# Attention outputs stored by row, the second block's fetch and spread moved behind the last weights, the second group's norms moved later (one core, four alternating layers)

## The chip, the cores and the metric

The kernel runs on one core of a Trainium2 chip. The metric is the device time of one launch in microseconds: the median of 3 runs. A profiled execution gives a page and a trace; its own time is given beside its span. Engines are called as the profile calls them: PE (matrix multiplies), DVE (vector), ACT (scalar activations), POOL (GpSimd), SP (here only an issuer of transfers). A transfer is issued by an engine's queue (SPq, POOLq, ACTq) and runs on 16 DMA engines.

## The reference, cut to what matters

A sequence of 2048 rows of 640 values goes through four layers, A, B, A, B (layer 0 to 3), each on a layer norm of its input and added to it.

```python
x = x + A(layernorm(x)); x = x + B(layernorm(x)); x = x + A(layernorm(x)); x = x + B(layernorm(x))

def A(x):                                   # 32 heads of 192
    for s in range(64):                     # 32 rows each
        h = concat([mem, x[32*s:32*s+32]])  # 8 + 32 rows
        q, k, v = h @ Wq, h @ Wk, h @ Wv
        o = softmax(mask(q k^T * scale)) v  # per head
        o = o @ Wo                          # summed over the heads
        mem = o[:8]; outs.append(o[8:])

def B(x):                                   # 32 heads of 20, over all 2048 rows
    q, k, v = split(x @ wqkv)
    phi(u) = concat(softmax(u @ w_phi), softmax(-u @ w_phi))
    kv = phi(k)^T v;  z = sum(phi(k))
    return (phi(q) kv / (phi(q) z + 1e-6)) @ wo
```

Layer A is sequential: a segment needs `mem` of the one before it. Of its 40 rows, only the first 32 (8 rows of `mem` and 24 outputs) are multiplied by Wo inside this chain. The last 8 rows of each segment, the "tails", feed nothing in the chain, and their product with Wo is made later, for 16 segments (128 rows) at once.

## The kernel before, in words

**Layer A** is a batch part (`A_pre`, the projections of the tail rows) and then the chain (`A_chain`, L918). A segment is worked off in 4 rounds of 8 heads, in the order 0 to 3 in even segments and 3 to 0 in odd ones, so that the weights of the last round serve the next segment's first. Weights stream from HBM on the SP queue: `load_slot` (L683) for Q, K and V, `load_wo` (L700) for the output weights, six pieces of 320 KB for a round. The chain's order is written out by hand (`manual_schedule`); instructions stand on each engine in program order there.

A round's attention (L1039) leaves its output in PSUM, 80 columns for two heads. Columns 0 to 63 are copied to `OT` (L1044 on ACT, L1045 on DVE) and multiplied by the output weights (`wo_round`, L1065). Columns 64 to 79, the tails, are copied by `keep_tail` (L1051 or L1053, and L1054) to `otb`, a tile with two buffers, and stored by `store_tail` (L1058) on the POOL queue: 128 partitions x 96 bf16 values, 24 KB, into `otb_d`, which is [segment, partition, 384]. That is done 4 x 64 times in a chain. The segment's last copies are `keep_rows` (L953, four on ACT), which wait for the result W of the four rounds and keep the 24 output rows.

**The end of the chain.** In segment 63, behind the first `wo_round`, SP issues `fetch_tails` (L1221) for block 0 and block 1 (a block is 16 segments: 128 partitions x 16 x 384 values, 1536 KB), then the six pieces of Wo for the last round, then six pieces of Wo of round 3 that layer B's beginning needs. Behind the last attention, `spread_tails` of block 0 (four copies of 128 x 1536, helper lines L87 on DVE and L89 on ACT) puts the fetched values into the order that the multiply needs. The spread of block 1 belongs to layer B, whose order a scheduler makes; it may place it among the chain's last steps.

**Layer B** (L247 on) begins with these tails: `multiply(tb)` for tb = 0 to 3, each of 48 chunks with a 512-column (L1251) and a 128-column (L1252) matmul; the sums of one block go to `obB` and from there to `attn`. Two buffers hold two blocks in turn, so fetch and spread of tb + 2 follow multiply of tb. Then come four groups of 512 rows (g = 0 to 3):

- `norm_T(g)`: load rows (L350), add the attention (L356, POOL), layer norm (`ln_moments`, `ln_deviation`, `ln_apply`: DVE L222, L224, L226, L240, L242; ACT L233, L234, and L244 for the rows), and turn them by PE (L166) and ACT (L89).
- `keys_values(g)`: for 4 blocks of 128 rows, keys on PE (L410, ps_pk), exponentials on ACT (L424), sums and reciprocals on DVE (L426, L428), values on PE (L410, ps_v), scaled on DVE (L437), and their products summed on PE (L443).
- `query_norms(g - 1)`: PE L473 and L481, ACT L345, L338, L339, DVE L340, L476, L482. `queries(g)`: PE L462, ACT L465.

Group 0's rows are normed and turned between multiply(2) and multiply(3); group 1's `norm_T` is held back by `issue_after` until group 0's last turn. `issue_after(i)` tells the scheduler not to place what follows before instruction i has been issued; it is about the order, not a wait on the chip. After the groups come the attention (PE L561, L564; ACT L566, DVE L567) and the output rows (PE L410 with ps_wo, DVE L596). Layer 1 also norms its output rows for the next layer A: `measure_rows` (the moments) and `finish_rows` (the rest), hung by `issue_after` behind the attention's steps of the next group. Layer 3 has no such norm.

The lines that the change touches are `otb_d` (L653), `store_tail` (L1058), `fetch_tails` (L1221), its calls at L1169, the spread in L493, `norm_T(1)` at L519, and `attention`, `measure_rows`, `finish_rows` and `output_rows` (L554 to L613).

Of the kernel before, what the change touches and what calls it, by code (L numbers as in the profile page):

```python
# [115 lines left out]
class Kernel:  # L116
# [131 lines left out]
    def layer_B(self, x_dram, at_dram, xout_dram, xnext_dram, li, bp, post):  # L248
# [42 lines left out]
        with tc.tile_pool(name=f"B{li}_kv", bufs=1, space=bass.MemoryType.PSUM, reuse_waits="tile") as kvp, \  # L291
# [121 lines left out]
            def keys_values(g, xnT):  # L413
                VS = DH * (512 // DH)

                def tokens(b):
# [3 lines left out]
                def keys(b):  # L420
                    ek = eks.next().rearrange("p (s d) -> p s d", s=2)
                    for ps, lo, hi in pair("ps_pk", 512, KC, tokens(b), lambda k, lo, hi: wqkv[:, k, D + lo:D + hi]):
                        for sg in range(2):
                            nc.scalar.activation(out=ek[:, sg, lo:hi], in_=ps[:, 0:hi - lo], func=ACT.Exp, scale=1.0 - 2.0 * sg)  # L424
                    sk = bp.tile([P, 2 * H], F32, name="sk", tag="sk")
                    nc.vector.reduce_sum(out=sk[:], in_=ek[:, :, :].rearrange("p s (h f) -> p (s h) f", f=DH), axis=AX.X)  # L426
# [22 lines left out]
                for b in range(4 * g, 4 * g + 4):  # L449
                    now = (b, *keys(b))  # L450
                    if before is not None:
                        values(*before)
                    before = now
                values(*before)

# [35 lines left out]
            with tc.issue_after(last.ins):  # L491
                load_rows(0)
            ow.append(spread(1, ot[1]))  # L493
            ot += [fetch(tb) for tb in range(2, 4)]
# [16 lines left out]
            turned = []  # L511
            multiply(3, ow[3], kv_ps[1], side_bank("ps_post"),
                     {35 + 4 * b: lambda b=b: turned.append(turn_rows(b, rows[b], first_xnT)) for b in range(4)})
            turned = turned[-1]
            waiting = None
            for g in range(NG):
                if g == 0:
                    xnT = first_xnT
                elif g == 1:  # L519
                    with tc.issue_after(turned.ins):  # L520
                        xnT = norm_T(g)
                else:
                    xnT = norm_T(g)
                if g == 1:
                    late_constants()
                keys_values(g, xnT)
# [27 lines left out]
            def attention(g, hl):  # L554
                tk = slice(512 * g, 512 * g + 512)
                oT = oTs.next().rearrange("p (c t) -> p c t", c=NC_)
                for c in range(NC_):
                    mc = sizes[c]
                    pn = bank("ps_num")
                    for sg in range(2):  # L560
                        nc.tensor.matmul(pn[0:mc, :], lhsT=kvm[0:mc, sg, c, 0:mc], rhs=phi[0:mc, sg, c, tk], start=(sg == 0),  # L561
                                         stop=(sg == 1))
                    pe = bank("ps_e")
                    nc.tensor.matmul(pe[0:mc, :], lhsT=expc[0:64, c, 0:mc], rhs=hl, start=True, stop=True)  # L564
                    rx = rxs.next()
                    spread = nc.scalar.activation(out=rx[0:mc, :], in_=pe[0:mc, :], func=ACT.Copy)  # L566
                    scaled = nc.vector.tensor_tensor(out=oT[0:mc, c, :], in0=pn[0:mc, :], in1=rx[0:mc, :], op=ALU.mult)  # L567
                    with tc.issue_after(spread.ins), tc.issue_after(scaled.ins):
                        if c in (0, 2):
                            measure_rows()  # L570
                        if c > 1:
                            finish_rows()
                return oT

            written, measured = [], []

            def measure_rows():
                if written:
                    ob, rows = written.pop(0)
                    measured.append((ob, self.ln_moments(bp, ob, 6), rows))  # L580

            def finish_rows():
                if measured:
                    ob, m, rows = measured.pop(0)
                    xn = xns.next()
                    self.ln_apply(bp, ob, m, self.ln_deviation(bp, m), xn, True)
                    nc.gpsimd.dma_start(out=xnext_dram[rows, :], in_=xn[:])

            def output_rows(g, oT):
                for b in range(4 * g, 4 * g + 4):  # L590
# [7 lines left out]
                    if xnext_dram is not None:  # L598
                        written.append((ob, rows))
                        if b < 4 * g + 2:  # L600
                            measure_rows()

            hl = [denominators(0, side_bank), denominators(1, bank)]
            for g in range(NG):
# [5 lines left out]
                output_rows(g, oT)  # L610
            for _ in range(4):
                measure_rows()
                finish_rows()  # L613
# [31 lines left out]
    def layer_A(self, xn_dram, at_dram, li, x_raw=None):  # L645
# [6 lines left out]
        self.vb_d = dram.tile([NSEG, NR, 2, 8, 896], BF16, name=f"vb{li}")  # L652
        self.otb_d = dram.tile([NSEG, P, 384], BF16, name=f"otb{li}")  # L653
        wview = self.wview
# [263 lines left out]
    def A_chain(self, xn_dram, at_dram, li, load_slot, piece, load_wo, late_wo, wo_mid, wo_end, low):  # L918
# [3 lines left out]
        with tc.tile_pool(name=f"A{li}_ch", reuse_waits="tile", bufs=1) as sp, \  # L922
# [28 lines left out]
            def keep_rows(W):  # L951
                for g in range(4):
                    nc.scalar.activation(out=orow[:, 160 * g:160 * g + 160], in_=W[32 * g:32 * g + 32, 0:160], func=ACT.Copy)  # L953

# [93 lines left out]
            def keep_tail(o, late=False):  # L1048
# [3 lines left out]
                else:  # L1052
                    nc.scalar.activation(out=otb[:, 0:3, :], in_=o[0][:, :, 64:80], func=ACT.Copy)  # L1053
                nc.vector.tensor_copy(out=otb[:, 3:6, :], in_=o[1][:, :, 64:80])  # L1054
                return otb

            def store_tail(otb, s, r):
                nc.gpsimd.dma_start(out=self.otb_d[s, :, 96 * r:96 * r + 96], in_=otb[:, :, :].rearrange("p c t -> p (c t)"))  # L1058

# [59 lines left out]
            for s in range(NSEG):  # L1119
# [30 lines left out]
                for n in range(L):  # L1150
# [63 lines left out]
                store_tail(keep_tail(o), s, order[L])  # L1214
# [81 lines left out]
```

## Time and profile before

| | |
|---|---|
| median of 3 runs | 3639.28 us (3635.94, 3639.28, 3642.32) |
| profiled execution | 3645.08 us, span 3643.3 us, mean granted clock 0.986 |
| PE busy | 3508.5 us (96%) |
| DVE, ACT, POOL busy | 2329.6, 2041.1, 1584.8 us (64%, 56%, 43%) |
| DMA | 933.32 MB, 256 GB/s over the span |
| stores L1058 | 512 of 24.0 KB, 4.8 us from issue to landing |
| fetches L1221 | 8 of 1536.0 KB, 12.1 us from issue to landing |
| first multiply of layers 1 and 3 (L1251) | begins at 1560.10 and 3384.7 us |

Each row of the timeline is the start, the length, the engine, the line, the instruction with its output and input, and in brackets how long the engine had been idle before it and what ended that. In a list of waits the numbers are the microseconds in total, how many times, and the longest. PE may be busy and still slow: the granted clock says at which share of full speed it ran. The layers' borders are seen in the slices of the page: the two stretches with hardly any DMA are the layers B.

### The profile page before, as it was taken

Reading aid. Unit: us, or ns where it says so; the run is one execution under the profiler, and the core shown is the slowest. Engines: PE = TensorE matmul, PEld = TensorE weight load, DVE = VectorE, ACT = ScalarE, POOL = GpSimd, SP = SyncE. Lnnn points to the kernel's source line nnn. Section 1 sums busy time; section 2 is a strip of 40 time slices with the busy share of each in tenths; the row PEclk is TensorE's granted clock in tenths of the full one; section 3 lists DMA queues with packets and bytes.
Section 4 is the critical chain, followed back from the end, with each engine's and each line's share of the span. In section 5 each row is a group of like instructions: output and inputs, shape, how many; then the busy total and the mean of one; then the engine's idle time right before and its main releaser. Section 6 shows DMA issues by size and latency. Waiting matters only on the chain.

```text
span 3643.3 us, 168559 instructions
## 1 busy us (share of the span) xinstructions
PE 3508.5 (96%) x70978; PEld 2274.2 (62%) x71269; DVE 2329.6 (64%) x6368; ACT 2041.1 (56%) x5233; POOL 1584.8 (43%) x4149
## 2 busy tenths in 40 slices
PE   9999999999999999989999899999999999999899
PEld 7766666666666666655377566666666666666553
DVE  5456666666666666646543566666666766666464
ACT  3356666666666666646432566666666666666362
POOL 3445555555555545530123445555555555555300
PEclk9999999999999999999899999999999999999998
DMA  9988888887888888860487888888887888888600
GB/s 306 328 292 292 285 281 277 291 295 270 287 292 281 277 281 289 285 207 1 140 270 211 296 272 292 288 278 290 285 288 270 294 291 276 281 293 281 202 1 29
DMA packets 533265, 933.32 MB, mean 256 GB/s; under 512 B 141066, under 2 KB 300442, under 8 KB 532506
## 3 DMA queue, kind: packets, MB, share of 16 engines
q1 hardware_dynamic: 431098, 821.50, 64.7%
q0 software_dynamic: 67744, 87.80, 8.3%
q10 hardware_dynamic: 33664, 13.24, 1.4%
q8 instruction: 557, 9.13, 1.0%
q14 instruction: 202, 1.65, 0.1%
HBM read 852.43 MB, written 73.73 MB: 254 GB/s over the span
## 4 chain that ended last, share of the span: by engine, by line
PE 67%; DMA 11%; issue 8%; DVE 7%; ACT 4%; POOL 2%; SPq 0%; POOLq 0%; DVEq 0%; ACTq 0%
PE ps_qk L989 19%; PE ps_w L1065 8%; PE ps_v L989 8%; DMA arena<-wo_rows 6%; PE ps_pre L880 6%; PE ps_o L1039 5%; PE ps_s L1031 4%; PE ps_pre L904 3%; PE ps_s L1097 3%; DVE hT L945 2%; PE ps_s L1026 2%; PE ps_idle L1072 2%; PE kv L1251 2%; DMA arena<-in_A_Wv_dram 2%; ACT raw L999 2%
## 5 line engine op out<-in xcount | busy, mean ns | idle before, releaser
L989 PEld LDWEIGHTS <-hT 128*32 128x32 bf16 x30720 | 738.2, 96 | 432.2 <-DVE hT L1213 28.4
L989 PE MATMUL ps_qk<-arena,hT 128*32 128x384 bf16 x20480 | 997.4, 327 | 10.6 <-DMA arena<-in_A_Wk_dram 1.8
L999 ACT ACTIVATE raw<-ps_qk 128x384 bf16<-128x384 f32 x1024 | 503.0, 491 | 380.4 <-PE ps_s L1097 241.0
L1065 PE MATMUL ps_w<-arena,OT 128*32 128x160 bf16 x24576 | 547.8, 235 | 52.2 <-DMA arena<-wo_rows 19.9
L972 POOL DMA_DIRECT2D Vp<-vb x512 | 259.1, 506 | 652.0 <-PE ps_o L1039 450.8
L989 PE MATMUL ps_v<-arena,hT 128*32 128x384 bf16 x10240 | 535.4, 329 | 5.9 <-DMA arena<-in_A_Wv_dram 5.9
L1065 PEld LDWEIGHTS <-OT 128*32 128x32 bf16 x24576 | 436.5, 97 | 149.6 <-issue 58.4
L1004 DVE STREAM_TRANSPOSE KT<-raw 128x384 bf16<-128x384 bf16 x512 | 296.1, 578 | 198.4 <-ACT raw L999 194.4
L1007 DVE STREAM_TRANSPOSE QT<-raw 128x256 bf16<-128x256 bf16 x512 | 227.9, 445 | 238.2 <-ACT raw L999 196.6
L960 POOL DMA_DIRECT2D kqb<-kqb x512 | 291.9, 570 | 174.6 <-POOL KT L968 147.3
L1020 DVE CAST Vp<-ps_v 64x384 bf16<-64x384 f32 x512 | 286.1, 559 | 96.2 <-ACT Vp L1018 81.6
L1058 POOL DMA_DIRECT2D otb<-otb x512 | 284.5, 556 | 131.1 <-DVE otb L1054 101.7
L1018 ACT ACTIVATE Vp<-ps_v 64x384 bf16<-64x384 f32 x512 | 246.3, 481 | 151.8 <-PE ps_v L989 114.1
L1045 DVE CAST OT<-ps_o 128x192 bf16<-128x192 f32 x512 | 183.1, 358 | 211.8 <-PE ps_o L1039 193.9
L1104 DVE TENSOR_TENSOR E<-E,ps_s 80x320 bf16<-80x320 bf16 x512 | 247.5, 483 | 73.2 <-ACT ps_s L1103 69.2
L1083 ACT ACTIVATE E<-ps_s 80x320 bf16<-80x320 f32 x512 | 221.9, 433 | 124.7 <-PE ps_s L1031 96.5
L1039 PEld LDWEIGHTS <-Vp 80*128 80x128 bf16 x4096 | 183.5, 99 | 154.4 <-issue 120.1
L1039 PE MATMUL ps_o<-E,Vp 80*128 80x80 bf16 x4096 | 233.8, 202 | 22.2 <-ACT Vp L1018 3.8
L1044 ACT ACTIVATE OT<-ps_o 128x192 bf16<-128x192 f32 x512 | 167.8, 328 | 146.1 <-PE ps_o L1039 146.1
L1031 PE MATMUL ps_s<-QT,KT 128*80 128x80 bf16 (+1 forms) x3072 | 232.7, 213 | 11.9 <-DVE KT L1004 3.4
L953 ACT ACTIVATE Vp<-ps_w 32x160 bf16<-32x160 f32 x512 | 150.7, 294 | 166.4 <-DVE wt L1212 151.2
L1072 PE MATMUL ps_idle<-arena,ident 128*128 128x230 bf16 (+1 forms) x1792 | 236.3, 260 | 0.0
(151 smaller groups left out, 5182.1 us busy)
## 6 DMA issues: line engine op xcount, KB each, us to landing
arena<-wo_rows SPq DMA_DIRECT2D x792, 320.0 KB, 6.9
arena<-in_A_Wq_dram SPq DMA_DIRECT2D x427, 384.0 KB, 4.6
arena<-in_A_Wv_dram SPq DMA_DIRECT2D x427, 384.0 KB, 6.4
arena<-in_A_Wk_dram SPq DMA_DIRECT2D x768, 192.0 KB, 4.9
kqb<-kqb POOLq DMA_DIRECT2D x512, 48.0 KB, 5.1
arena<-in_A_Wk_dram SPq DMA_DIRECT2D x43, 384.0 KB, 7.4
vb<-arena POOLq DMA_DIRECT2D x128, 112.0 KB, 6.0
Vp<-vb POOLq DMA_DIRECT2D x512, 28.0 KB, 4.8
```

Of the source, the lines that this page charges most:

```text
L960: nc.gpsimd.dma_start(out=kqb[:], in_=self.kqb_d[s, :, r, :])
L972: nc.gpsimd.dma_start(out=Vs[n % 2][64:80, :], in_=self.vb_d[s, r].rearrange("g t f -> (g t) f"))
L989: nc.tensor.matmul(o[32 * g:32 * g + 32, 0:384], lhsT=hT[:, b, :], rhs=rhs, start=(i == 0), stop=(i == KC - 1), tile_position=(0, 32 * g), ...
L999: nc.scalar.activation(out=raw[:], in_=ps[:, 0:384], func=ACT.Copy)
L1004: nc.vector.transpose(out=KT[:, :, 0:64], in_=raw[:, :].rearrange("p (c j) -> p c j", j=64))
L1020: nc.vector.tensor_copy(out=o, in_=i)
L1031: nc.tensor.matmul(S[0:80, c0:c0 + 80 * (q1 - q0)], lhsT=KT[:, 3 * x + i, :], rhs=QT[:, x, q0:q1, :], start=False, stop=(x == 1 and i == 2 ...
L1039: nc.tensor.matmul(O[x][:, 80 * i:80 * i + 80], lhsT=Vs[n % 2][0:80, 448 * x + k:448 * x + k + 128], rhs=E[0:80, 160 * x + 80 * e:160 * x ...
L1058: nc.gpsimd.dma_start(out=self.otb_d[s, :, 96 * r:96 * r + 96], in_=otb[:, :, :].rearrange("p c t -> p (c t)"))
L1065: nc.tensor.matmul(W[32 * g:32 * g + 32, 0:160], lhsT=OT[:, c, q:q + 32], rhs=w[:, 640 * i + 160 * g:640 * i + 160 * g + 160], start=(firs ...
L1072: nc.tensor.matmul(ps[:, 0:w], lhsT=self.ident[:, :], rhs=wo_mid[:, 0:w], start=True, stop=True, skip_group_check=True)
L1104: nc.vector.tensor_tensor(out=E[0:80, 0:320], in0=E[0:80, 0:320], in1=rc, op=ALU.mult)
```

## The change

Four edits.

1. `otb_d` is laid out [partition, segment, 384]. A store's 128 pieces of 192 bytes then stand 49,152 bytes apart, where they stood 768 apart. A fetch reads 128 runs of 12,288 bytes, where it read 2048 of 768.
2. The fetch of block 1 stands on the SP queue behind all twelve pieces of Wo. The spread of block 1 is placed behind the chain's last tail copy on DVE and the last copy of `keep_rows` on ACT.
3. `norm_T(1)` is held until the last exponential and the last sum of group 0's second block, not only until group 0's last turn.
4. The norm of layer 1's output: the moments follow the output rows directly, the rest of the norm follows each attention step from the second on, with no `issue_after`, and what is left is done at the end.

```diff
-            ow.append(spread(1, ot[1]))
+            with tc.issue_after(self.chain_end[0].ins), tc.issue_after(self.chain_end[1].ins):
+                ow.append(spread(1, ot[1]))
...
                 elif g == 1:
-                    with tc.issue_after(turned.ins):
+                    with tc.issue_after(self.second_block[0].ins), tc.issue_after(self.second_block[1].ins):
                         xnT = norm_T(g)
...
-                    with tc.issue_after(spread.ins), tc.issue_after(scaled.ins):
-                        if c in (0, 2):
-                            measure_rows()
-                        if c > 1:
-                            finish_rows()
+                    if c > 0:
+                        finish_rows()
...
-                        written.append((ob, rows))
-                        if b < 4 * g + 2:
-                            measure_rows()
+                        unfinished.append((ob, self.ln_moments(bp, ob, 6), rows))
...
-            for _ in range(4):
-                measure_rows()
+            while unfinished:
                 finish_rows()
...
-        self.otb_d = dram.tile([NSEG, P, 384], BF16, name=f"otb{li}")
+        self.otb_d = dram.tile([P, NSEG, 384], BF16, name=f"otb{li}")
...
-                nc.gpsimd.dma_start(out=self.otb_d[s, :, 96 * r:96 * r + 96], in_=otb[:, :, :].rearrange("p c t -> p (c t)"))
+                nc.gpsimd.dma_start(out=self.otb_d[:, s, 96 * r:96 * r + 96], in_=otb[:, :, :].rearrange("p c t -> p (c t)"))
...
                             if s == NSEG - 1:
-                                tails = [self.fetch_tails(tb, low) for tb in range(2)]
+                                tails = [self.fetch_tails(0, low)]
                             load_wo(order[L])
                             if s == NSEG - 1:
                                 load_wo(3, low[:, 0:7680])
+                                tails.append(self.fetch_tails(1, low))
...
-        self.nc.sync.dma_start(out=ot, in_=self.otb_d[16 * tb:16 * tb + 16].rearrange("s p f -> p s f"))
+        self.nc.sync.dma_start(out=ot, in_=self.otb_d[:, 16 * tb:16 * tb + 16, :])
```

On the engines, by the order of the two programs: at the chain's end, ACT has L1044 (the last OT), two L89 of block 0's spread, L1053, four L953 and then the two L89 of block 1; before, one L89 of block 1 stood ahead of L1044 and one behind L1053. DVE has L1045, two L87, L1054 and then the two L87 of block 1; before, these stood ahead of L1045. In group 0 of layer B the L424s on ACT stand without L244s between them, and the norms of group 1 stand behind group 0's queries; on PE ten L473 and two more then stand between the turns of group 1 and ahead of its first pk, where three stood. In layer 3 edit 4 changes nothing.

More of the change, by code (lines that the diff above doesn't have):

```diff
@@ L414, in keys_values @@
                 VS = DH * (512 // DH)
+                exps, sums = [], []
                 def tokens(b):
@@ L423, in keys @@
                         for sg in range(2):
-                            nc.scalar.activation(out=ek[:, sg, lo:hi], in_=ps[:, 0:hi - lo], func=ACT.Exp, scale=1.0 - 2.0 * sg)
+                            exps.append(nc.scalar.activation(out=ek[:, sg, lo:hi], in_=ps[:, 0:hi - lo], func=ACT.Exp, scale=1.0 - 2.0 * sg))
                     sk = bp.tile([P, 2 * H], F32, name="sk", tag="sk")
-                    nc.vector.reduce_sum(out=sk[:], in_=ek[:, :, :].rearrange("p s (h f) -> p (s h) f", f=DH), axis=AX.X)
+                    sums.append(nc.vector.reduce_sum(out=sk[:], in_=ek[:, :, :].rearrange("p s (h f) -> p (s h) f", f=DH), axis=AX.X))
                     rk = bp.tile([P, 2, H], F32, name="rk", tag="rk")
@@ L453, in keys_values @@
                     before = now
+                    if b == 4 * g + 1:
+                        self.second_block = exps[-1], sums[-1]
                 values(*before)
@@ L510, in layer_B @@
             first_xnT = new_xnT()
-            turned = []
             multiply(3, ow[3], kv_ps[1], side_bank("ps_post"),
-                     {35 + 4 * b: lambda b=b: turned.append(turn_rows(b, rows[b], first_xnT)) for b in range(4)})
-            turned = turned[-1]
+                     {35 + 4 * b: lambda b=b: turn_rows(b, rows[b], first_xnT) for b in range(4)})
             waiting = None
@@ L565, in attention @@
                     rx = rxs.next()
-                    spread = nc.scalar.activation(out=rx[0:mc, :], in_=pe[0:mc, :], func=ACT.Copy)
-                    scaled = nc.vector.tensor_tensor(out=oT[0:mc, c, :], in0=pn[0:mc, :], in1=rx[0:mc, :], op=ALU.mult)
-                    with tc.issue_after(spread.ins), tc.issue_after(scaled.ins):
-                        if c in (0, 2):
-                            measure_rows()
-                        if c > 1:
-                            finish_rows()
-                return oT
[L575 to L580, printed above, removed]
+                    nc.scalar.activation(out=rx[0:mc, :], in_=pe[0:mc, :], func=ACT.Copy)
+                    nc.vector.tensor_tensor(out=oT[0:mc, c, :], in0=pn[0:mc, :], in1=rx[0:mc, :], op=ALU.mult)
+                    if c > 0:
+                        finish_rows()
+                return oT
+            unfinished = []
             def finish_rows():
-                if measured:
-                    ob, m, rows = measured.pop(0)
+                if unfinished:
+                    ob, m, rows = unfinished.pop(0)
                     xn = xns.next()
@@ L952, in keep_rows @@
                 for g in range(4):
-                    nc.scalar.activation(out=orow[:, 160 * g:160 * g + 160], in_=W[32 * g:32 * g + 32, 0:160], func=ACT.Copy)
+                    last = nc.scalar.activation(out=orow[:, 160 * g:160 * g + 160], in_=W[32 * g:32 * g + 32, 0:160], func=ACT.Copy)
+                self.chain_end.append(last)
             def store_rows(s):
@@ L1053, in keep_tail @@
                     nc.scalar.activation(out=otb[:, 0:3, :], in_=o[0][:, :, 64:80], func=ACT.Copy)
-                nc.vector.tensor_copy(out=otb[:, 3:6, :], in_=o[1][:, :, 64:80])
+                self.chain_end = [nc.vector.tensor_copy(out=otb[:, 3:6, :], in_=o[1][:, :, 64:80])]
                 return otb
             def store_tail(otb, s, r):
-                nc.gpsimd.dma_start(out=self.otb_d[s, :, 96 * r:96 * r + 96], in_=otb[:, :, :].rearrange("p c t -> p (c t)"))
+                nc.gpsimd.dma_start(out=self.otb_d[:, s, 96 * r:96 * r + 96], in_=otb[:, :, :].rearrange("p c t -> p (c t)"))
             def wo_round(W, r, OT, first, last):
@@ L1213, in A_chain @@
                         nc.vector.tensor_copy(out=hT[:, b0:b1, 0:8], in_=wt[:, b0:b1, 0:8])
-                store_tail(keep_tail(o), s, order[L])
+                otb = keep_tail(o)
+                store_tail(otb, s, order[L])
                 keep_rows(W)
```

## The prediction

> **What bounds the kernel now.** I read the page from the top: the busy shares, the chain that ended last, then the waits of the stretches that the change touches.
>
> ```profile
> PE 3508.5 (96%) x70978; PEld 2274.2 (62%) x71269; DVE 2329.6 (64%) x6368; ACT 2041.1 (56%) x5233; POOL 1584.8 (43%) x4149
> ...
> PE 67%; DMA 11%; issue 8%; DVE 7%; ACT 4%; POOL 2%; SPq 0%; POOLq 0%; DVEq 0%; ACTq 0%
> ```
>
> PE is busy 96% of 3643.3 us, so 134.8 us of its idle time and the clock are all that can be won without taking work away. The largest single hole is where the chain hands over to layer B. The waits of that stretch (1545 to 1560 us):
>
> ```profile
> PE ps_w L1065 <- ACT OT L1044: 6.9, 1, 6.9
> ACT arena L89 <- DMA arena<-otb: 6.8, 1, 6.8
> DVE arena L87 <- DMA arena<-otb: 6.8, 1, 6.8
> ...
> PE ps_w L1065 <- DMA arena<-wo_rows: 1.1, 3, 0.4
> ```
>
> and its timeline (start, length, engine, line):
>
> ```profile
> 1547.92 0.66 PE L1072 MATMUL ps_idle<-arena,ident 128*128 128x230 bf16 x5
> 1553.71 1.03 DVE L87 COPY arena<-arena 128x1536 bf16<-128x1536 bf16 x2 [6.78 <-DMA arena<-otb]
> 1553.72 1.49 ACT L89 ACTIVATE arena<-arena 128x1536 bf16<-128x1536 bf16 x1 [6.78 <-DMA arena<-otb]
> 1554.66 0.35 DVE L1045 CAST OT<-ps_o 128x192 bf16<-128x192 f32 x1
> ...
> 1555.12 0.31 ACT L1044 ACTIVATE OT<-ps_o 128x192 bf16<-128x192 f32 x1
> ...
> 1555.48 1.27 PE L1065 MATMUL ps_w<-arena,OT 128*32 128x160 bf16 x24 [6.90 <-ACT OT L1044]
> ...
> 1558.78 0.46 PE L1065 MATMUL ps_w<-arena,OT 128*32 128x160 bf16 x8 [0.37 <-DMA arena<-wo_rows]
> ...
> 1560.10 0.63 PE L1251 MATMUL kv<-arena 128*128 128x512 bf16 x1
> ```
>
> The second block's spread (L87, L89) stands ahead of the two OT copies on DVE and ACT and waits for the second fetch, landed at 1553.62. PE can't go on until those copies are done. When they are, the last round is paced by its weight pieces, which land 0.83 us apart until 1558.78. Both causes have to go to win anything: without the spread in front, PE would only wait for the pieces. The same stands at 3370 to 3385 in the second chain (5.8 us for the copy).
>
> **Part 1: the fetches (layout, order, spread).** DMA is full here (busy share 1.08 from 1548.6 to 1555.4), so a piece lands when the bytes ahead of it are through. One fetch is 2048 packets of 768 B at 41 ns over 16 engines: 2048 x 41 / 16 = 5.25 us. With the second fetch behind the twelve pieces, the sixth piece lands 5.25 us earlier: 1558.78 - 5.25 = 1553.5. With rows of 12,288 B the first fetch needs fewer, larger packets; packets of 3072 B in this trace take 121 to 142 ns, so 512 x 121 to 142 / 16 = 3.9 to 4.5 us, 2,560 B ones at 102 to 110 ns make at most 4.9. That is 0.4 to 1.4 us less; I take 0.9. The sixth piece lands at 1552.6. The OT copies no longer wait for a fetch: they come behind L1039 at about 1548.1 to 1548.7, and the first block's spread, due when fetch 0 lands (1548.27 before), is off the path. The round's last eight matmuls start with the sixth piece; from there to the first L1251 it was 1560.10 - 1558.78 = 1.3 us, so 1553.9 instead of 1560.10: **-6.2 us**, -5.0 to -7.7 from the bounds (a round limited by copies, a cheaper fetch). Twice, for two chains: **-12.4**.
>
> What is late next: fetch 1 lands after the twelve pieces, about 1552.6 + 6 x 0.83 + 4 = 1561.6; the spread is two L89 of 1.48 (ACT) beside two L87 of 0.5 (DVE): done by 1565. multiply(1) starts one multiply (14.8 us, 1560.10 to 1574.92) behind multiply(0), at about 1568.7. So 4 us of cover; each us beyond is a us. Those copies now stand ahead of obB's (L1254, L1255) on their engines, which are wanted only at 1568. Fetch 2 and the weights of layer B come later on the SP queue in the order, not in time, since the bytes ahead are the same or cheaper.
>
> The granted clock was 0.50 from 1553.3 to 1563.5 behind the hole; a multiply takes 14.82 us there, 13.29 in layer 3 at full clock: 1.5 us. A shorter hole (still 4 us) may or may not spare it; I count nothing. [...]
>
> **Part 2: stores at a stride of 49,152 B.** 512 stores L1058, now 128 pieces of 192 B, 48 KiB apart, instead of 768 B.
>
> ```profile
> otb<-otb POOLq DMA_DIRECT2D x512, 24.0 KB, 4.8
> ...
> arena<-otb SPq DMA_DIRECT2D x8, 1536.0 KB, 12.1
> ```
>
> They matter only by their landing: ACT's copy L1053 of the last round waits for the store two turns before:
>
> ```profile
> ACT otb L1053 <- DMA otb<-otb: 87.8, 115, 2.1
> ```
>
> Behind it ACT is idle for a median of 1.06 us until L953 needs the last round's result, so about 1 us of a later landing is free; beyond that each of some 126 segments pays. The trace does show stores at large strides: the 384 B pieces of kqb go 196,608 B apart at 24.2 ns each, on the line of the packets at small strides, and the 112 KB vb stores (1792 B rows 114,688 B apart) land in 6.0 us. I take **0**, bounds 0 and +4; the rest is a rival. [...]
>
> **Part 3: norms of group 1 behind group 0's second block** (both B layers). Gone are L244s of 0.95 us between the L424s of group 0:
>
> ```profile
> PE ps_v L410 <- ACT arena L424: 3.8, 3, 1.6
> ```
>
> These three stalls (1.64, 1.28, 0.89) lie in 1625 to 1642. DVE is nearly as busy there (22.0 of 28.8 us up to 1654.6), so I count half: -1.8. But the norms come back at the boundary to group 1. By the order of the two programs, ACT does between its last L465 and its first L424 of group 1 only four L89 now (2.47 us):
>
> ```profile
> 1653.49 2.47 ACT L89 ACTIVATE arena<-ps_x 128x640 bf16<-128x640 bf16 x4
> ...
> 1654.55 2.89 PE L410 MATMUL ps_pk<-arena 128*128 128x512 bf16 x20
> ...
> 1657.52 1.49 DVE L426 TENSOR_REDUCE sk<-arena 128x64 f32<-128x1280 bf16 x1 [5.49 <-ACT arena L424]
> ```
>
> After, it does four L89 (0.70 each), three L244 (0.95), four pairs of L233 and L234 (0.31 + 0.21), two L345 (0.60), L338 and L339 (0.62, 0.63): 2.8 + 2.9 + 2.1 + 1.2 + 1.25 = 10.2 us, some 9.6 with their overlap. So about 7 us later for the first L426 of group 1. PE fills some of it: nine L473 (0.33 apiece, 3.0 us) are moved there from behind, and with group 1's first rows later the PE waits some 4 us beyond what the L473 cover. In the stretch after it PE has 29.5 busy of 30.2 us, so that nothing is caught up. Walking PE and ACT through by their rows, the first pk (L410) of group 2 comes 64 to 65.3 us behind that of group 0, instead of 60.7 (59.0 plus five L473 of group 1's norms that stood behind it and now stand ahead): +4, with the gain taken off; bounds -1.8 (PE finds all its work) and +7 (none). Two layers: **+8**.
>
> **Part 4: norms of layer 1's output in its place, no late issue.** Only layer 1 has them. ACT meets L244 in front of L566 in groups 1 to 3; I find -0.5, +1.6 and -0.1 from the orders, and -1.5 at the end, where the last rows are done sooner: **0**, bounds -3 and +3.
>
> **Sum.** -12.4 + 0 + 8 + 0 = -4.4: 3645.08 of the profiled execution becomes 3640.7. The median is 5.8 below that execution, 3639.28 - 4.4 = 3634.9, so **3635**. A difference of 0.2% (7.3 us) is about what a measurement of this kernel can tell from no change.
>
> **Rivals.** *First: the boundary costs nothing.* the L473 and transposes that move there, and DVE's earlier sums, cover the later norms; then -12.4 and 0 to -3.6 more, so 3623 to 3627. For it: PE's waits at the boundary are now small (nothing over 0.6 between 1640 and 1662). Against: the ACT sum above. 27%. *Second: the boundary takes all,* +7 a layer with a shorter gain in part 1: -10 + 14 = +4, 3638 to 3645. For it: an idle of 3 us and more was followed by the half clock at 1553. 20%. *Third, on the slower side: the stores land later.* Place: L1053 in each of 126 segments; it decides from 1.06 us above the present 4.8: each 0.1 us beyond costs 126 x 0.1 = 12.6 us, so +2 us in the landing costs 118, +1.2 some 18. From -4.4 it is slower than before by a rise of some 1.1, and over the 0.2% by 1.2. For it: the stores' pieces now stand in 128 places far apart, and a packet now holds eight pieces (1536 B, 73 ns). Against: kqb's pieces. 13%, 3650 to 3760.
>
> **How the numbers follow.** Forecast 40% (3630 to 3640), first rival 27%, second 20%, third 13%. The range takes in the first rival's end with part 4's bound (3620) and the start of the third's, 3655; about 2 in 10 lies outside, mostly above. Faster by over 0.2% (under 3632): the first rival and a quarter of the forecast, 0.38; slower (over 3646.6): the third and part of the second, 0.18; within: 0.44.
>
> **What would show it.** Right: no wait of L1065 for OT at the chain's end, L87 of the spread behind L1054, first L1251 some 6 us earlier after each chain; L1053's wait on otb as now (87.8 us); ACT between the last L465 and first L424 of group 1 some 9 us, a PE wait at ps_pk there. Wrong: store landings above 5.9 us, PE waiting for the second spread at multiply(1), or no PE wait at the boundary.

## The result, and the profile after

The changed kernel takes **3653.03 us** (median of 5 runs, 3651.88 to 3659.41), the kernel before 3639.22 us beside it: a ratio of 1.0044, interval 1.0029 to 1.0058. The forecast was 3635, faster. The profiled execution has a span of 3651.2 us (3643.3 before).

At the chain's end the profile shows what was forecast. (The changed kernel's lines have other numbers; there L1031, L1036, L1045, L1046, L1057 and L1245 are the L1039, L1044, L1053, L1054, L1065 and L1251 of before, and in layer B L425, L427, L438, L444, L465, L468, L476, L484, L485 and L568 are L424, L426, L437, L443, L462, L465, L473, L481, L482 and L566.) PE's main wait from 1540 to 1555 us (in all, how often, the longest), and the timeline there:

```profile
PE ps_w L1057 <- DMA arena<-wo_rows: 2.8, 5, 0.7
```

```profile
1542.66 0.33 ACT L1036 ACTIVATE OT<-ps_o 128x192 bf16<-128x192 f32 x1 [0.48 <-PE ps_o L1031]
...
1547.61 0.46 PE L1057 MATMUL ps_w<-arena,OT 128*32 128x160 bf16 x8 [0.75 <-DMA arena<-wo_rows]
...
1549.47 0.63 PE L1245 MATMUL kv<-arena 128*128 128x512 bf16 x1
...
1556.72 1.03 DVE L87 COPY arena<-arena 128x1536 bf16<-128x1536 bf16 x2 [12.42 <-DMA arena<-otb]
1556.77 2.86 ACT L89 ACTIVATE arena<-arena 128x1536 bf16<-128x1536 bf16 x2 [7.44 <-issue]
```

The wait of 6.9 us for OT is gone, the copy comes at once behind the attention, and the pieces of wo_rows alone pace the last round. The second spread is done at 1559.6, well ahead of the second multiply (1564.26). The stores land as before:

```profile
otb<-otb POOLq DMA_DIRECT2D x512, 24.0 KB, 4.7
arena<-otb SPq DMA_DIRECT2D x8, 1536.0 KB, 10.7
```

Now the four groups of the first layer B, each line a group from its first pk to the next (the last up to the last pq). Before, then after:

```profile
1625.80:1654.60 28.80, 24.88 (x184) 14.91 (x183) 22.03 (x66) 18.93 (x52) 7.84 (x7) 1.00 0.14 39
1654.60:1684.80 30.20, 29.51 (x194) 15.96 (x193) 20.18 (x45) 20.83 (x49) 0.00 (x0) 1.00 0.00 1
1684.80:1714.40 29.60, 29.47 (x196) 15.78 (x196) 19.49 (x38) 19.38 (x41) 0.00 (x0) 1.00 0.01 1
1714.40:1742.30 27.90, 27.48 (x178) 14.75 (x176) 22.09 (x61) 14.68 (x33) 0.00 (x0) 1.00 0.14 43
```

```profile
1615.20:1649.10 33.90, 27.68 (x192) 16.03 (x192) 28.92 (x79) 20.13 (x48) 7.78 (x7) 1.00 0.11 32
1649.10:1680.20 31.10, 29.03 (x190) 15.99 (x189) 20.67 (x49) 18.85 (x46) 0.00 (x0) 0.95 0.01 2
1680.20:1716.10 35.90, 32.82 (x200) 17.00 (x202) 20.70 (x45) 22.44 (x50) 0.00 (x0) 0.95 0.00 0
1716.10:1742.30 26.20, 24.64 (x166) 14.21 (x166) 19.89 (x55) 13.25 (x30) 0.00 (x0) 1.00 0.14 46
```

The columns are the stretch, its length, busy time of PE, PE's loads, DVE, ACT and POOL (with the number of instructions), then the clock, the busy share of the DMA engines and GB/s. Group 0 is 5.1 us longer and group 2 another 6.3; only 1.7 come back in group 3. In group 0 DVE has 6.9 us more to do. In groups 1 and 2 the clock is 0.95. PE's waits in 1615 to 1743 are then:

```profile
PE ps_v L410 <- ACT arena L425: 4.9, 6, 1.1
PE ps_x L166 <- ACT arena L244: 2.3, 1, 2.3
PE ps_sq L476 <- ACT arena L345: 1.9, 2, 1.2
PE ps_e L484 <- DVE arena L485: 1.3, 2, 0.8
PE kv L444 <- DVE arena L438: 1.1, 2, 0.7
```

With two small ones this makes 11.9 us, where it was 4.8 before (4.2 for L424 and 0.6 for L437): 7.1 more. The two stretches of 3.41 us at a granted clock of 0.50 add up to 3.4, an estimate that takes PE as busy all through them. Together that is 10.5 of the 10.6 us.

Stage by stage, read off the two timelines (us; "chain" is from its first L1039 to its last, "chain end" is from the last L1039 to the first L1251 of the second multiply, "groups" from the first pk to the last pq, "attention" from the first L561 to the last L410 of the output rows; behind the bar the time at half clock):

| | chain 1 | chain end, layer 1 | groups, layer 1 | attention, layer 1 | chain 3 | chain end, layer 3 | groups, layer 3 | attention, layer 3 |
|---|---|---|---|---|---|---|---|---|
| before | 1370.6 | 26.9 / 10.2 | 116.5 / 0 | 86.7 / 27.3 | 1368.0 | 25.3 / 10.2 | 116.1 / 0 | 80.6 / 23.9 |
| after | 1365.1 | 21.7 / 6.8 | 127.1 / 6.8 | 94.2 / 34.1 | 1366.5 | 20.9 / 3.4 | 126.4 / 6.8 | 79.4 / 17.1 |
| after - before | -5.5 | -5.2 | +10.6 | +7.5 | -1.5 | -4.4 | +10.3 | -1.2 |

These columns sum to +10.6, the stretches between them to -2.7, and the span is 7.9 longer. Of the 2.7, the gap between the groups and the attention gives 1.1 in each layer (3.5 us before, 2.4 after). (The medians differ by 13.8; the chains, which the change hardly touches, scatter, as the experiments show.)

### The profile page after: what moved, and what is told of

Its sections match the earlier page's. It is cut to its first block, busy times and chain, and to the rows that moved or that the text cites. A ratio compares the mean times of both kernels' runs of the same rounds, so it can differ in the third digit from the quotient of the medians.

```text
span 3651.2 us, 168550 instructions
## 1 busy us (share of the span) xinstructions
PE 3508.7 (96%) x70944; PEld 2278.0 (62%) x71269; DVE 2332.0 (64%) x6368; ACT 2039.9 (56%) x5233; POOL 1577.8 (43%) x4149
## 4 chain that ended last, share of the span: by engine, by line
PE 69%; DMA 11%; DVE 8%; ACT 6%; issue 3%; PEld 2%; POOL 1%; SPq 0%; DVEq 0%; POOLq 0%; ACTq 0%
PE ps_qk L981 20%; PE ps_w L1057 8%; PE ps_v L981 8%; DMA arena<-wo_rows 6%; PE ps_o L1031 5%; PE ps_s L1023 4%; PE ps_pre L871 3%; PE ps_s L1089 3%; DVE hT L936 2%; PE kv L1245 2%; PE ps_s L1018 2%; PE ps_idle L1064 2%; ACT raw L991 2%; DMA arena<-in_A_Wv_dram 2%; PE ps_pre L895 2%
## 5 line engine op out<-in xcount | busy, mean ns | idle before, releaser
L1057 PE MATMUL ps_w<-arena,OT 128*32 128x160 bf16 x24576 | 544.4, 234 | 32.7 <-DMA arena<-wo_rows 19.7
L1057 PEld LDWEIGHTS <-OT 128*32 128x32 bf16 x24576 | 435.2, 97 | 128.1 <-issue 50.6
L1031 PEld LDWEIGHTS <-Vp 80*128 80x128 bf16 x4096 | 183.4, 99 | 158.1 <-issue 123.4
L1031 PE MATMUL ps_o<-E,Vp 80*128 80x80 bf16 x4096 | 234.0, 202 | 25.1 <-DMA Vp<-vb 5.3
L1036 ACT ACTIVATE OT<-ps_o 128x192 bf16<-128x192 f32 x512 | 167.8, 328 | 144.5 <-PE ps_o L1031 144.3
```

The source lines that it names most:

```text
L1031: nc.tensor.matmul(O[x][:, 80 * i:80 * i + 80], lhsT=Vs[n % 2][0:80, 448 * x + k:448 * x + k + 128], rhs=E[0:80, 160 * x + 80 * e:160 * x ...
L1057: nc.tensor.matmul(W[32 * g:32 * g + 32, 0:160], lhsT=OT[:, c, q:q + 32], rhs=w[:, 640 * i + 160 * g:640 * i + 160 * g + 160], start=(firs ...
```

## The experiments

**The edits in layer B undone, one and both, and the layout alone**, each timed beside the kernel before.

```diff
# a_norms_early: in the changed kernel (`turned` is kept again, as before)
...
-                    with tc.issue_after(self.second_block[0].ins), tc.issue_after(self.second_block[1].ins):
+                    with tc.issue_after(turned.ins):
                         xnT = norm_T(g)
```
```diff
# a_out_before: in the changed kernel, as before
-                    if c > 0:
-                        finish_rows()
+                    with tc.issue_after(spread.ins), tc.issue_after(scaled.ins):
+                        if c in (0, 2):
+                            measure_rows()
+                        if c > 1:
+                            finish_rows()
...   # and measure_rows and its calls in output_rows and at the end, as before
```
```diff
# a_both_undone: both of these.   b_layout: in the kernel before, only
+        self.otb_d = dram.tile([P, NSEG, 384], BF16, name=f"otb{li}")
...   # and the store and the fetch that go with it, as in the change
```

> The changed kernel with one edit undone: group 1's norms are held only until group 0's last turn, as before. Theory (the late norms put ACT work in front of the first exponentials of groups 1 and 3, PE waits there, and the clock drops behind the waits; 10.6 us from group 0's first pk to the last pq in layer 1, 10.9 in layer 3): 3653 - 21 = 3632 us, and no PE wait on L244 at the boundary to group 1. Rival (the boundary's loss comes from the earlier start of layer B or from transfers, not from this edit): 3647 to 3653.

> The changed kernel with the norm of layer 1's output put back as before (moments and the rest late, behind attention steps). Theory (this edit costs 7.5 us in layer 1, by waits of ps_wo for ACT L568 and one more stretch at half clock): 3653 - 7.5 = 3645.5. Rival (these waits belong to the profiled execution, or are moved work): 3651 to 3653.

> The changed kernel with both edits in layer B undone; what is left is the store layout, the late second fetch and the late spread. Theory (the parts add up): 3653 - 21 - 7.5 = 3624.5, that is some 15 under the kernel before, of which 9.5 at the two chain ends and the rest in the chains. Rival (the chains' gain of 7 in one execution is its scatter): 3630.

> The kernel before with the stored outputs laid out by row, and nothing else. Theory A (the layout makes the chain itself faster: 5.6 us in the first chain, 1.5 in the second, since the stores L1058 land earlier and ACT waits less at L1053): 3639 - 7 - up to 2 for the cheaper fetches = 3630 to 3632, with the gain spread over the 64 segments. Theory B (scatter of one execution): 3637 to 3639.

| | time, before beside it | ratio (interval) | chain ends | groups | attention, layer 1 |
|---|---|---|---|---|---|
| a_norms_early | 3638.82, 3651.41 | 0.9963 (0.9951 to 0.9976) | 19.8, 21.7 | 116.4, 117.6 | 92.2 |
| a_out_before | 3661.44, 3651.41 | 1.0026 (1.0016 to 1.0037) | 19.3, 18.1 | 129.9, 128.7 | 89.2 |
| a_both_undone | 3638.01, 3651.41 | 0.9965 (0.9947 to 0.9984) | 21.2, 19.9 | 116.4, 116.6 | 90.3 |
| b_layout | 3647.55, 3651.41 | 0.9988 (0.9974 to 1.0003) | 23.7, 24.5 | 116.3, 117.9 | 85.3 |

The kernel before is slower beside these than it was in the first comparison, so ratios count, not the expected microseconds. With the hold taken back the groups are at 116 to 118 us again and the ratio falls from 1.0044 to 0.9963: the hold is the larger part. Both undone wins against the kernel before. The last edit alone is not resolved by ratios here: with it undone beside the hold 1.0044 becomes 1.0026, with intervals that overlap, and with it undone where the hold is gone nothing changes (0.9963, 0.9965). The layout alone is within its interval of no change; in one execution its 62 whole intervals of each chain (from segment 1 to segment 63) took 1325.2 and 1326.7 us, where the kernel before had 1322.5 and 1322.3. So theory A falls: no gain in the chain comes with the layout, and the changed kernel's fast first chain was scatter.

**Which of fetch and spread opens the chain's end, and does a smaller hold help** (one execution each).

```diff
# b_fetch_late: in the kernel before
-                                tails = [self.fetch_tails(tb, low) for tb in range(2)]
+                                tails = [self.fetch_tails(0, low)]
...
+                                tails.append(self.fetch_tails(1, low))
```
```diff
# b_spread_late: in the kernel before
+            with tc.issue_after(self.chain_end[0].ins), tc.issue_after(self.chain_end[1].ins):
+                ow.append(spread(1, ot[1]))
# a_both_unlayout: these two together.   a_gate_first: in the changed kernel
-                    if b == 4 * g + 1:
+                    if b == 4 * g:
                         self.second_block = exps[-1], sums[-1]
```

> The kernel before with the second fetch behind the twelve weight pieces, and nothing else; the second spread still stands ahead of the OT copies. From the chain's last attend (L1039) to the first L1251 it was 12.2 us in layer 1 and 11.5 in layer 3 before, and 6.9 and 7.3 after the change. Theory (both the fetch and the spread have to move, since the spread in front makes PE wait for whatever fetch it needs): the second fetch now lands some 4 to 6 us later, so PE waits longer: 16 to 19 us. Rival (the bytes ahead of the weights are the whole cause): 7 us.

> The kernel before with the second spread behind the chain's last copies, and nothing else; the second fetch still stands ahead of the weights. Theory (the last round is then paced by the pieces, of which the sixth landed at 1558.78 where the multiply began at 1560.10): 11 to 12 us from the last L1039 to the first L1251, as before, though the wait for OT is gone. Rival (the spread in front is the whole cause): 7 us.

> The kernel before with the second fetch late and the second spread late, the stored outputs laid out as before, layer B as before. Theory (the fetch of 768-byte pieces costs 0.4 to 1.4 us more ahead of the weights, the rest of the gain is the order): 7.3 to 8.5 us from the last L1039 to the first L1251. Rival (the layout is what gives the gain, since it alone took 1.9 and 1.3 us off): 10 us or more.

> The changed kernel with group 1's norms held until the last exponential and sum of group 0's first block, not the second. From group 0's first pk to the last pq it takes 116.5 us in layer 1 and 116.1 in layer 3 before, 127.1 and 126.4 after. Theory (what is lost is the lead that the norms have over the groups, so the loss grows with the delay and comes back at later groups): between, 118 to 124 us. Rival (any hold behind group 0's exponentials costs the whole, since the scheduler then orders all later norms anew): 126 to 127.

From the last L1039 to the first multiply: b_fetch_late 8.5 and 6.7 us, b_spread_late 11.4 and 12.3, a_both_unlayout 7.5 and 7.0. In b_spread_late the wait for OT has turned into one for the pieces, as expected:

```profile
PE ps_w L1067 <- DMA arena<-wo_rows: 6.6, 6, 4.5
```

b_fetch_late went against the theory. The trace tells why: with the fetch late, the scheduler places the spread behind the chain by itself.

```profile
1544.72 0.33 ACT L1044 ACTIVATE OT<-ps_o 128x192 bf16<-128x192 f32 x1 [0.84 <-PE ps_o L1039]
...
1551.81 1.21 ACT L953 ACTIVATE Vp<-ps_w 32x160 bf16<-32x160 f32 x4 [3.92 <-PE ps_w L1065]
1561.14 2.86 ACT L89 ACTIVATE arena<-arena 128x1536 bf16<-128x1536 bf16 x2 [8.11 <-issue]
```

The instructions of b_fetch_late and a_both_unlayout stand in the same order on ACT, DVE, POOL and SP, so the edit of the spread does nothing once the fetch is late. The two are in effect one program, and took 3625.96 and 3621.57 us on the same chip (the kernel before 3635.80): 4.4 us is scatter. With the layout, over all runs with the late fetch, the stretch was 5.2 to 7.3 us at 18 chain ends (mean 6.4), without it 6.7 to 8.5 at six (mean 7.3): some 1.0 us for the cheaper first fetch, between means whose ranges overlap.

a_gate_first took 126.9 and 129.4 us for the groups (3661.21, the kernel before 3635.80). A hold until the first block costs as much as one until the second, so the graded theory falls. The moments (L222) stand nearly alike in both: behind group 0's last L438 come seven of group 1's eight (all eight in the changed kernel) and all of groups 2 and 3.

**What of the hold costs, and which half of the last edit** (one execution each).

```diff
# a_moments_early: in the changed kernel, group 1
+                    with tc.issue_after(turned.ins):
+                        load_rows(g)
+                        measured = [moments_of(b) for b in range(4 * g, 4 * g + 4)]   # load, add, L222 to L226
                     with tc.issue_after(self.second_block[0].ins), tc.issue_after(self.second_block[1].ins):
-                        xnT = norm_T(g)
+                        ...   # L233 to L244 and the turn for each b
# a_no_hold: in the changed kernel, norm_T(1) with no issue_after
```
```diff
# n_moments_direct: in a_both_undone (measure_rows and its calls go)
...
-                        written.append((ob, rows))
-                        if b < 4 * g + 2:
-                            measure_rows()
+                        measured.append((ob, self.ln_moments(bp, ob, 6), rows))
# n_finish_free: in a_both_undone (measure_rows stays held)
...
-                        if c > 1:
-                            finish_rows()
+                    if c > 0:
+                        finish_rows()
```

> The changed kernel with group 1's norms split: loads, sums and moments (DVE L222 to L226) are held only until group 0's last turn, as before; the rest (L233, L234, L240 to L244) and the turns until the second block, as in the change. Group 0's first pk to the last pq took 116.5 and 116.1 us before, 127.1 and 126.4 after the change. Theory (the cost is that the moments lose their place beside the last multiply, where DVE is idle, and come behind 18 us of full DVE work): 116 to 119. Rival (the cost is the ACT work that the late L244 put ahead of group 1's first exponentials, wherever the moments stand): 122 to 127.

> The changed kernel with no hold on group 1's norms at all. If the norms' only good place is beside the last multiply, where the hold of before puts them, 116 to 117 us from group 0's first pk to the last pq, and the last multiply unchanged (14.3 us from its start to the first pk). Rival (without a hold they stand ahead of group 0's own norms or the multiplies' copies): the last multiply or the two before take 2 us or more longer.

> Fetch, spread and layout as changed, norms of group 1 as before; of the last edit only one half: the moments of layer 1's output rows follow the rows directly, the rest stays held behind the attention's steps from the third on. In layer 1 from the first attention matmul to the last output matmul it took 83.4 to 90.3 us in seven kernels with the old order and 92.2 to 94.2 in three with the new. Theory (the costly half is the other one: L244 and L233 without a hold stand in front of L568 on ACT): 84 to 89. Rival (DVE's moments in front of the output rows' sums delay PE): 91 to 94.

> The other half: the moments of layer 1's output rows held as before, the rest of the norm from the second attention step on with no hold. Theory: 91 to 94 us from the first attention matmul to the last output matmul of layer 1. Rival: 84 to 89.

| | time, before 3647.03 | groups / half clock | attention, layer 1 / half clock |
|---|---|---|---|
| a_moments_early | 3634.88 | 120.9 / 3.4, 118.8 / 0 | 88.2 / 27.3 |
| a_no_hold | 3643.24 | 118.7 / 0, 118.0 / 0 | 92.3 / 34.1 |
| n_moments_direct | 3631.18 | 116.5 / 0, 116.2 / 0 | 86.5 / 30.7 |
| n_finish_free | 3634.00 | 117.8 / 3.4, 117.0 / 0 | 84.4 / 27.3 |

With the moments early and the late L244 kept, most of the loss is gone (10.6 to 4.4 us in layer 1, 10.3 to 2.7 in layer 3): 118.8 in layer 3 as the theory had it, in layer 1 120.9, in which one stretch of 3.41 us at half clock lies (up to 1.7, an estimate from 3.41 us at 0.50). The second loss, ahead of group 3, vanishes whole (0.04 us in both layers); some 2.5 us at the boundary to group 1 remain for the late L244, so the rival holds for a quarter. Before, the moments of groups 1 and 2 stood beside the last multiply; group 1's begin with the second of the two in the first row here, and group 2's end with the second row, ahead of group 0's first sum:

```profile
1615.69 0.88 DVE L222 BATCH_NORM_STATS2 ln_stats<-arena 128x6 f32<-128x320 bf16 x2
...
1624.62 1.21 DVE L222 BATCH_NORM_STATS2 ln_stats<-arena 128x6 f32<-128x320 bf16 x3
1630.67 2.88 DVE L426 TENSOR_REDUCE sk<-arena 128x64 f32<-128x1280 bf16 x2 [1.56 <-ACT arena L424]
```

DVE has room for them there. Without them it is busy for 6.96 of 14.30 us beside the last multiply, with them for 14.02 of 14.20, and the multiply takes 14.3 us either way. The kernel before, then the changed one, from the start of the last multiply to the first pk:

```profile
1611.60:1625.80 14.20, 14.20 (x118) 8.44 (x117) 14.02 (x50) 7.37 (x17) 7.52 (x13) 1.00 0.51 155
```

```profile
1600.90:1615.20 14.30, 14.14 (x115) 8.52 (x117) 6.96 (x26) 7.39 (x17) 7.64 (x13) 1.00 0.50 156
```

After, they all begin behind group 0's last scaling, and from its first sum to there (1618.2 to 1633.8) DVE is busy for 15.60 of 15.60 us:

```profile
1618.19 2.88 DVE L427 TENSOR_REDUCE sk<-arena 128x64 f32<-128x1280 bf16 x2 [2.12 <-ACT arena L425]
...
1632.22 1.70 DVE L438 TENSOR_TENSOR arena<-ps_v,rk 128x500 bf16<-128x500 f32 x4
1633.83 1.27 DVE L222 BATCH_NORM_STATS2 ln_stats<-arena 128x6 f32<-128x320 bf16 x3
```

Without a hold nothing is won either (118.7 and 118.0 us; the last multiply takes 14.4 and 14.3 us, unchanged). With the hold of before the groups took 115.9 to 117.9 us in all eleven kernels that have it, so it is the best of the three, by little against none.

Of the last edit neither half costs anything that shows (86.5 and 84.4 us, where nine executions with the old order took 83.4 to 90.3), so the theory that the unheld L244 do it by themselves fell. With both halves three L244 in a row stand on ACT in front of the fifth L568 of the attention of groups 1 and 2, and two in group 3, and PE waits for what follows with its output rows. Before, such a row of three stood once, in front of the last L566 of group 1. PE's longest wait there before, then after, with the ACT rows behind one of the three waits:

```profile
PE ps_wo L410 <- ACT arena L566: 2.6, 2, 1.9
```

```profile
PE ps_wo L410 <- ACT arena L568: 5.6, 3, 2.2
```

```profile
1792.07 2.53 ACT L244 ACTIVATE arena<-arena,ln_shift,ln_rstd 128x640 bf16<-128x640 bf16 x3
1794.50 0.57 ACT L568 ACTIVATE arena<-ps_e 120x512 f32<-120x512 f32 x1
```

All of PE's waits in this attention make 6.4 us before and 10.1 after. The wait for the output rows is 5.6 in a_norms_early, a_moments_early, a_no_hold and b_out_only too, which have the new order. Their attention lengths still spread (88.2 to 94.2 us in six executions, mean 92.2, against a mean of 86.9 in the nine with the old order), in part because the time at half clock differs (27.3 us with 88.2, 34.1 with 92.2 to 94.2).

**Each edit alone, in the kernel before, timed.** The diffs are those of the change, one edit at a time (b_fetch_only is b_fetch_late).

> The kernel before with group 1's norms held until group 0's second block, and nothing else. If this edit is the cause of the loss by itself: 126 to 130 us from group 0's first pk to the last pq in both layers (116.5 and 116.1 before), two or more stretches at half clock in each, and 20 to 27 us in all: a ratio of 1.0055 to 1.0075. If it only costs together with the earlier start of layer B: 116 to 120 and a ratio within 1.002.

> The kernel before with only the second fetch behind the weights, timed. By the traces the chain ends take 4.2 and 4.8 us less and nothing else changes: 9 us, a ratio of 0.9975. If what looked like 10 to 20 us in single executions were real: 0.995 or less. If the chains' scatter hides a loss: 0.999 or more.

> The kernel before with only the last edit, the norm of layer 1's output without holds. If it costs by itself: 92 to 94 us from the first attention matmul to the last output matmul of layer 1 (86.7 before), all else unchanged, a ratio of 1.001 to 1.0025. If it only costs with the other edits: 83 to 90 us and a ratio of 0.9995 to 1.0005.

| | ratio (interval) | chain ends | groups | attention, layer 1 |
|---|---|---|---|---|
| b_norms_only | 1.0063 (1.0038 to 1.0089) | 26.9, 26.8 | 126.4, 125.6 | 90.1 |
| b_fetch_only | 0.9984 (0.9967 to 1.0000) | 21.7, 20.8 | 116.5, 116.6 | 85.3 |
| b_out_only | 1.0014 (0.9997 to 1.0032) | 26.7, 26.5 | 116.3, 116.6 | 92.2 |

In the stages each edit does by itself what it did in the whole: the hold costs about 10 us a layer, the fetch wins about 5 a chain, and layer 1's attention is 5.5 longer with the unheld norms (92.2 against 86.7, of which the waits show some 4). The three ratios add up to 1.0061. That lies above the interval of the measured 1.0044, but the three intervals together leave some 0.0035 to either side, which takes it in. In whole times only the cost of the hold is clear; the ratios of the other two reach 1.

The best versions are the change without the hold (a_norms_early, 0.9963) and without both edits in layer B (a_both_undone, 0.9965); the runs don't tell them apart.

## Why the prediction was wrong, point by point

- **Part 1, right in mechanism, a little large.** Forecast -6.2 a chain (-5.0 to -7.7); the stretch from the last L1039 to the first multiply is 5.3 and 4.2 shorter in the profiled execution, the second outside the bounds. Over all executions its mean is 12.3 us where the chain's end is that of before (six chain ends) and 6.4 where fetch and layout are changed (eighteen): some 6 less. The spread's own edit, which I counted as needed, was not: the scheduler does it. The 0.9 for the cheaper first fetch came out near (some 1.0), but with some luck: I had it from packets of 3072 and 2560 B, and 2560 B at 110 ns would have made 4.2 us, not at most 4.9. The fetches of the changed kernel run in packets of 12,288 B at 471 ns, 128 x 471 / 16 = 3.8 us, 1.5 less by that sum. The clock, for which I counted nothing, gave nothing: the first multiply took 14.7 and 13.8 us before, 14.8 and 13.6 after. (By the rows my 14.82 is 14.72; a multiply at full clock, layer 3's second, took 13.13, not 13.29.)
- **Part 2, right.** Landings took 4.7 us against 4.8 before; L1053's wait on otb 83.0 us in all against 87.8. The stores' packets are the same in both traces, 8192 of 1536 B at 73 ns. The third rival did not happen, and no run shows a cost of the 48-KiB stride.
- **Part 3, the step that failed: the sum ended at the first pk of group 2, and what the hold does behind it was put at nothing.** Forecast +4 a layer, +7 at most; measured +10.6 and +10.3. As far as I walked, the length was right: the first pk of group 2 comes 65.0 and 64.5 us behind that of group 0, where the walk had 64 to 65.3. Against the walk's base, with the five L473 that moved ahead, this is +4.3 and +4.2. That the 4 came out is in part luck: one stretch at half clock lies in it in each layer, worth up to 1.7 (an estimate from 3.41 us at 0.50), of which the walk had none, so the waits were smaller than walked. ACT took some 9.4 us between its last L468 and its first L425 of group 1, as forecast; PE waited there, but at the turns (2.3) and at L476, the L473 of before (1.9), not at ps_pk. Behind it I said that nothing is caught up, and did not go on to the next boundary. There the lateness came back, +6.3 and +6.1 ahead of group 3, and only 1.7 was regained in group 3, though ten L473 and two L481 fewer are left for it. The moments of groups 1 and 2 had lost their place beside the last multiply and those of all groups followed one another; with the moments alone put back (a_moments_early) this second loss is gone. I had counted the L244 that ACT does at the boundary and put no price on DVE's moments, which were free only where they stood. The second rival, which named the clock, also ended at +7.
- **Part 4, wrong.** Forecast 0 (-3 to +3) from the order on ACT; layer 1's attention took 7.5 us longer in the profiled pair, and 5.3 between the means of all executions. PE's waits grew by 3.7 us, which my count of the stalls had at nothing. The rest is clock, for which I had no term: 34.1 us at half clock against 27.3, some 3 us at the 0.44 a us that is read below in layer 3 (an estimate). In whole times this cost is not resolved (1.0014, 0.9997 to 1.0032).
- **Sum.** Up to the second multiply -9.6, then 0 + 20.9 + 7.5: +18.8 in place of -4.4. The chains and layer 3's attention, which the edits hardly touch, gave 8.2 back in this execution, and 2.7 lie between the stages: +7.9.

## What to carry to other kernels

When a piece of work is held later, look first at what it stood beside: work that costs nothing in an idle stretch of its engine can have a price elsewhere (the last multiply took 14.20 us with the moments beside it and 14.30 without, and without them there group 2 became 6.3 us longer). Follow the delay through every later turn of the loop, not only to the first boundary, because what depends on the same engine order can slide with it: here +4.3 us at the first pk of group 2 were followed by another 6.3 at that of group 3. And when two releases of held work are each free, their sum need not be (layer 1's attention took 86.5 and 84.4 us with one half of the last edit, 92.2 with both).

## What the runs showed of the hardware that was not expected

- The granted clock fell to 0.50 behind short waits too; in the kernel before it had fallen 4.7 us into the wait of 6.9 us for OT (at 1553.3). Stretches at half clock came in steps of 3.41 us in the changed kernel, on one grid (1553.57, where the clock came back, to 1649.15 are 28 steps, from there to 1710.59 are 18); the one at 1649.1 and the one at 1710.6 follow a step in which PE was busy for 1.11 and 2.06 of 3.40 us:

```profile
1645.70:1649.10 3.40, 1.11 (x13) 0.71 (x13) 1.83 (x7) 3.05 (x6) 0.00 (x0) 1.00 0.00 0
1707.20:1710.60 3.40, 2.06 (x14) 0.91 (x13) 1.78 (x4) 3.21 (x5) 0.00 (x0) 1.00 0.00 0
```

  PE waited once for 2.3 us in the first of these steps, and for 0.6 and 0.8 us in the second; these are two cases, and no threshold can be read from them.
- What time at half clock cost can be read in layer 3's attention, whose instructions on ACT and DVE stand in the same order in all kernels without the hold: 13.7 us at half clock go with 76.1 us, 17.1 with 77.5, 23.9 with 80.6, which is 0.44 us for each (an estimate from these three). How much it is differs from execution to execution of one program (b_fetch_late 13.7, b_fetch_only 17.1 there), so a stage can differ by 4 us with no edit in it.
- The chains scatter by more than most edits are worth: the 62 whole intervals of one chain took between 1317.4 and 1331.2 us over all runs, in no relation to the edits. The groups came out at 115.9 to 117.9 us in all 22 stretches with the old hold and at 125.6 to 129.9 in the eight with the late one, so their loss of 10 us stands out in a single execution, and whole times need many runs to show it.
